# The product that turns the log-sums is laid out without the margin behind its rows

## The chip, the cores and the metric

The kernel runs on one core of one Trainium2 chip. The metric is the device time of one execution in microseconds; the other seven cores are idle. "PE" is the engine of the matrix products, "PEld" its weight loads, DVE, ACT and POOL the vector, scalar and general engines, SP the queue that issues transfers.

## The reference, cut to what matters

Two attention layers with separate inputs, side by side in the output. Each has 2048 positions, width 1024 and 32 heads of 32 columns; all numbers are float32.

```
def _B_ref(x, wqkv, wo):                       # "dense" here: a window of 256 keys
    q, k, v = ... (x @ wqkv) in 32 heads of 32
    scores = einsum("bhqd,bhkd->bhqk", q, k) * 32 ** -0.5
    mask = 0 <= query - key < 256
    p = softmax(where(mask, scores, -1e9))
    o = einsum("bhqk,bhkd->bhqd", p, v)
    return o @ wo

def _A_ref(x, wqkv, wo):                       # 8 keys per query, every second position
    ...
return concatenate([a, b], axis=-1)
```

Layer B is the one that the change concerns.

## The kernel before

The work is cut into eight units of 512 positions: units 0 to 3 are layer B (dense), units 4 to 7 layer A (window). A unit has eight groups of four heads; the 32 groups of the dense units are numbered 0 to 31 below (group = 8 x unit + number in the unit). All products of the projections are made of three products of rounded parts, high x high, high x low and low x high (`TERMS`), each 128 x 128 by 128 x 512 (or 256); they are the products named `g` in the profile and the bulk of PE's work.

A dense group goes twice over its scores, in products named `s` on a ring of four banks (`rs`):

- First pass (`first`, 16 products `s<-kst,qst`, queries on the partitions). DVE masks each product and takes its minimum after a change of sign (`nm`, line 1323), ACT exponentiates and sums (`sm`, line 1328). After the 16th, `log_sum` takes the logarithm on ACT (`ln`, line 1341), and DVE forms `nl` = `nm` - `ln` and splits it into a high and a low part (`hl`, lines 1346 to 1349).
- The product that turns the log-sums (`rows`): one product `s<-ident,hl` of `hl` with an identity. It brings the 128 x 32 numbers onto 32 partitions. Four DVE operations (line 1363, `spread`) write them, one for each head, as 32 more rows under the queries (`qst`, partitions 96 to 127). The matching rows of the keys hold ones, so that the second pass subtracts the log-sum in the product itself.
- Second pass (`second`, products `s<-qst,kst`, keys on the partitions). ACT exponentiates straight into `pbuf`, POOL or DVE mask it (`keep`, lines 1387 and 1390), and products named `o` multiply it with the values.

The order on every engine is written at build time by a planner. It keeps a model clock (`Clock`, `ck`) with a time at which each engine comes free, and has four lists: `aux` (the turning products alone), `ones` (first passes), `twos` (second passes and values) and `gemm` (the `g` products). At each step the item whose `ready()` is earliest goes to PE next, and `aux` wins a tie. Work for the other engines is put into their queues when the model clock reaches it; a `keep` goes to POOL or DVE, and a cast of weights to ACT or DVE, whichever the model has free first. On the chip each engine's instructions keep that order and wait for semaphores, so that the model's times decide nothing but the order. The item of `rows` is entered in `parts` with the condition that a bank of `rs` is free and that the model's end of `hl`, `e2`, has passed by a margin:

```
HL_LATE = 0.8
...
e2 = ck.use("dve", 0.52, e, port=True)
aux.append(Item(lambda: latest(rs.when(BANK_LATE), e2 + HL_LATE), lambda: rows(hl), 0.08))
```

The times of `spread`, and with them those of the second pass, are counted from the place where the turning product was laid.

Of the kernel before, what the change touches and what calls it, by code (L numbers as in the profile page):

```python
# [29 lines left out]
CHUNK, ASKED, LEFT, FETCHED = 256, 150, 290, 7.0  # L30
EXTRA, EACH = 246, 5.2
P_LATE = 1.5
HL_LATE = 0.8
VPARTS = ((0,4),(4,2),(6,2))
V_SLOTS = {0:0,5:1,7:2}
O_SLOTS = {2: (0, 1), 3: (2, 3), 4: (4, 5), 5: (6, 7)}
# [17 lines left out]
BANK_LATE = 0.0  # L54
# [189 lines left out]
def kernel(ctx, tc, xs, wqk, wv, wo, outs, units):  # L244
# [26 lines left out]
    def mm(out, left, right, **k):  # L271
        issued[0] += 4 if left.dtype == F32 else 2
        n = int(issued[0] + EXTRA - ASKED) // CHUNK
        if n > asked[0]:
            asked[:] = n, ck.now
        nc.tensor.matmul(out, left, right, **k)  # L276
# [195 lines left out]
    xt, xready, ot, rows, waiting = {}, {}, {}, {}, {}  # L472
# [24 lines left out]
    rg, rs, ro = Ring(psg, 7 - NS, "g"), Ring(pss, NS, "s"), Ring(pso, 1, "o")  # L497
# [7 lines left out]
    def latest(*ts):  # L505
        return None if any(t is None for t in ts) else max(ts)
# [788 lines left out]
    def attention(u, s):  # L1295
# [43 lines left out]
        def log_sum():  # L1339
            ln = small.tile([P, 16], F32, tag="ln", name="ln")  # L1340
            nc.scalar.activation(ln, h["sm"], AF.Ln)
            e = ck.use("act", 0.13, ck.now) - 0.03

            def parts():
                nl = small.tile([P, 16], F32, tag="nl", name="nl")
                nc.vector.tensor_tensor(nl, h["nm"], ln, op=ALU.subtract)
                hl = small.tile([P, 2, 16], F32R, tag="hl", name="hl")
                nc.vector.tensor_copy(hl[:, 0, :], nl)
                nc.vector.tensor_tensor(hl[:, 1, :], nl, hl[:, 0, :].bitcast(F32), op=ALU.subtract)
                e2 = ck.use("dve", 0.52, e, port=True)  # L1350
                aux.append(Item(lambda: latest(rs.when(BANK_LATE), e2 + HL_LATE), lambda: rows(hl), 0.08))

            ck.defer(e, parts)

        def rows(hl):
            ps, bank = rs.take()
            mm(ps[0:32, 0:P], hl.rearrange("p a b -> p (a b)"), cst["ident"], start=True, stop=True)

            def spread():

                h["rows"] = []
                for j in range(4):
                    nc.vector.tensor_tensor(q[96:P, j, :].rearrange("p (b s) -> p b s", s=P),  # L1363
                                            ps[0:32, None, 0:P].to_broadcast([32, 4, P]),
                                            cst["pick"][0:32, 4 * j:4 * j + 4, None].to_broadcast([32, 4, P]), op=ALU.mult)
                    e = ck.use("dve", 0.61, ck.now)
                    h["rows"].append(e + ROWS_LATE)
                rs.give(bank, e)

            return spread  # L1370
# [102 lines left out]
    aux, ones, twos, gemm = [], [], [], []  # L1473
# [121 lines left out]
```

## Time and profile before

| | us |
|---|---|
| median of 3 runs | 1811.09 (1808.05 to 1811.22) |
| the profiled execution | 1810.36 |
| its span, from the first to the last instruction | 1808.5 |
| PE busy | 1779.4 (98% of the span) |
| DVE, ACT, POOL busy | 1294.4, 935.2, 417.7 |
| granted clock of PE, mean | 0.998 |

A PE that is called busy may still be late: its products overlap, and their ends are modelled. What counts is when the next product starts. "Idle before" in a row is the time that an engine stood still ahead of the instructions of the group, with what ended it. Of the 1.9 us between span and time nothing is seen in the profile.

### The profile page before, as it was taken

The numbers are of one execution on the slowest core, as the hardware profiler recorded it, in microseconds if no ns is written. First come the engines' busy times: TensorE is split into PE (matmuls) and PEld (weight loads), VectorE is DVE, ScalarE is ACT, GpSimd is POOL, SyncE is SP. The second block draws the span as 40 slices with busy tenths as digits, with TensorE's granted clock in tenths as the row PEclk, the third lists the DMA queues.
The fourth block names the chain that finished last, engine by engine and source line by source line (L and its number), as shares of the span: only waits on it lengthen the run. The fifth ranks groups of instructions, "written<-read, shape, count | busy, mean of one in ns | idle before, by whom it ended". The sixth has DMA issues, their size and how long they took to land. (4 is left out here: it accounts for less than half of the span.)

```text
span 1808.5 us, 38436 instructions
## 1 busy us (share of the span) xinstructions
PE 1779.4 (98%) x14490; PEld 1439.0 (80%) x14490; DVE 1294.4 (72%) x2879; ACT 935.2 (52%) x2319; POOL 417.7 (23%) x967
## 2 busy tenths in 40 slices
PE   9999999999999999999999999999999999999999
PEld 7787778888777888777788788878887777887887
DVE  6777877768767668866678476665666768678866
ACT  5566466555666565655654543434443435356442
POOL 2323322232333233232324400110011101001220
PEclk9999999999999999999999999999999999999999
DMA  8455665645655556555556266666576568858984
GB/s 241 120 146 126 183 165 146 163 141 140 184 140 150 159 135 165 152 146 141 142 133 182 63 207 180 203 207 192 172 214 200 180 191 275 259 178 283 333 291 148
DMA packets 154649, 324.57 MB, mean 179 GB/s; under 512 B 18016, under 2 KB 58976, under 8 KB 154464
## 3 DMA queue, kind: packets, MB, share of 16 engines
q0 software_dynamic: 45792, 166.74, 30.5%
q1 hardware_dynamic: 97728, 134.40, 26.5%
q10 hardware_dynamic: 10944, 20.98, 3.1%
q8 instruction: 115, 1.88, 0.4%
q14 instruction: 70, 0.57, 0.1%
HBM read 201.33 MB, written 53.48 MB: 141 GB/s over the span
## 5 line engine op out<-in xcount | busy, mean ns | idle before, releaser
L276 PE MATMUL g<-x,w 128*128 128x512 f32 x3744 | 928.5, 395 | 5.1 <-ACT x L228 2.0
L276 PEld LDWEIGHTS g<-x,w 128*128 128x128 f32 x3744 | 692.0, 189 | 145.2 <-issue 5.6
L234 DVE TENSOR_TENSOR w<-raw,w 128x512 fp32r<-128x512 f32 x510 | 334.6, 697 | 51.7 <-ACT w L228 45.6
L276 PE MATMUL g<-w,x 128*128 128x256 f32 (+1 forms) x1872 | 332.8, 327 | 0.9 <-DVE w L234 0.7
L1323 DVE CUSTOM_DVE_ANT_0 s<-s,mask_d 128x384 f32<-128x384 f32 (+2 forms) x512 | 262.1, 553 | 98.1 <-PE s L276 96.8
L1328 ACT ACTIVATE s<-s,nm 128x384 f32<-128x384 f32 (+2 forms) x512 | 274.8, 538 | 101.4 <-DVE nm L1323 99.3
L276 PEld LDWEIGHTS g<-w,x 128*128 128x128 f32 x1872 | 276.7, 190 | 28.1 <-DVE w L234 2.2
L1387 POOL TENSOR_SCALAR_AFFINE_SELECT pbuf<-pbuf 128x128 f32<-128x128 f32 (+1 forms) x619 | 226.0, 393 | 300.9 <-ACT pbuf L1408 299.5
L1408 ACT ACTIVATE pbuf<-s 128x384 f32<-128x384 f32 (+2 forms) x480 | 202.7, 505 | 88.6 <-PE s L276 87.1
L276 PE MATMUL g<-r,w 128*128 128x512 f32 x768 | 190.8, 394 | 1.5 <-DVE r L1287 0.8
L276 PEld LDWEIGHTS g<-r,w 128*128 128x128 f32 x768 | 141.9, 188 | 30.9 <-DVE r L1287 1.8
L183 POOL DMA_DIRECT2D raw<-wqk x126 | 68.0, 540 | 417.2 <-DVE w L234 267.4
L276 PEld LDWEIGHTS s<-qst,kst 128*128 128x128 f32 x704 | 112.2, 189 | 43.6 <-ACT s L1328 17.7
L276 PE MATMUL s<-kst,qst 96*128 96x384 f32 (+2 forms) x512 | 142.9, 343 | 3.7 <-ACT s L1328 1.1
L231 DVE CAST w<-raw 128x1024 fp32r<-128x1024 f32 x176 | 122.1, 694 | 27.2 <-PE g L276 26.8
L276 PE MATMUL s<-qst,kst 128*128 128x256 f32 (+2 forms) x704 | 136.6, 302 | 4.6 <-ACT s L1328 3.5
L228 ACT CAST w<-raw 128x1024 fp32r<-128x1024 f32 (+1 forms) x80 | 82.7, 1038 | 75.8 <-PE g L276 29.0
L276 PEld LDWEIGHTS s<-kst,qst 96*128 96x128 f32 x512 | 92.9, 189 | 29.4 <-issue 6.1
L1328 ACT ACTIVATION_READ_ACCUMULATOR s<-s,nm 128x1 f32 x512 | 105.9, 207 | 0.0
L1190 ACT COPY wide<-band 32x512 f32<-32x512 f32 x128 | 79.0, 617 | 46.4 <-DVE band L1181 44.6
L276 PE MATMUL o<-pbuf,vbuf 128*32 128x384 f32 (+2 forms) x1408 | 91.1, 389 | 0.0
L1363 DVE TENSOR_TENSOR qst<-s,pick 32x512 fp32r<-32x512 f32 x128 | 79.3, 676 | 12.8 <-PE s L276 12.0
(90 smaller groups left out, 1327.7 us busy)
## 6 DMA issues: line engine op xcount, KB each, us to landing
raw<-wqk POOLq DMA_DIRECT2D x126, 512.0 KB, 4.6
raw<-wv POOLq DMA_DIRECT2D x60, 512.0 KB, 5.2
qst<-nat SPq DMA_DIRECT2D x96, 256.0 KB, 4.2
kst<-nat SPq DMA_DIRECT2D x96, 256.0 KB, 5.6
raw<-wo POOLq DMA_DIRECT2D x44, 512.0 KB, 4.9
raw<-xs POOLq DMA_DIRECT2D x28, 512.0 KB, 4.9
outs<-ost ACTq DMA_DIRECT2D x38, 256.0 KB, 2.8
kst<-halo SPq DMA_DIRECT2D x72, 128.0 KB, 4.5
```

The source lines that it names most:

```text
L183: (self.nc.scalar if early else self.nc.gpsimd).dma_start(raw if len(ap.shape) == 2 else raw.rearrange("p (a b) -> p a b", a=2), ap)
L228: nc.scalar.copy(t[:, 0, :], raw)
L231: nc.vector.tensor_copy(t[:, 0, :], raw)
L234: nc.vector.tensor_tensor(t[:, 1, c:c + 512], raw[:, c:c + 512], t[:, 0, c:c + 512].bitcast(F32), op=ALU.subtract)
L276: nc.tensor.matmul(out, left, right, **k)
L1190: nc.scalar.copy(diag[r:r + 32, :, :, c:c + 32], turned[r:r + 32, :, :, 1, :])
L1323: nc.vector.tensor_tensor_reduce(ps[:, :n], ps[:, :n], mask[:, cut:full], scale=-1.0, scalar=BIG, op0=ALU.add, op1=ALU.min, accum_out=nm)
L1328: nc.scalar.activation(ps[:, :n], ps[:, :n], AF.Exp, bias=nm, scale=-1.0, accum_out=sm)
L1363: nc.vector.tensor_tensor(q[96:P, j, :].rearrange("p (b s) -> p b s", s=P), ps[0:32, None, 0:P].to_broadcast([32, 4, P]), cst["pick"][0:32 ...
L1387: nc.gpsimd.affine_select(w, w, pattern=[[0, m], [step, n]], compare_op=ALU.is_ge, fill=0.0, base=base, channel_multiplier=chan)
L1408: nc.scalar.activation(w, ps[:, :pack * n].rearrange("p (j n) -> p j n", j=pack), AF.Exp)
```

## The change

The margin goes: the turning product may be laid down as soon as the model has `hl` ready.

```
-HL_LATE = 0.8
...
-                aux.append(Item(lambda: latest(rs.when(BANK_LATE), e2 + HL_LATE), lambda: rows(hl), 0.08))
+                aux.append(Item(lambda: latest(rs.when(BANK_LATE), e2), lambda: rows(hl), 0.08))
```

Line numbers from 33 on fall by one. No product is added or left out; the order shifts from the first turning product on. On PE the first 184 and the last 5,748 of 11,164 instructions of the order stand as before; on SP all do. On DVE there are 15 more instructions and on POOL 13 fewer, because a `keep` finds another engine free first: on 128 x 2 x 128 elements DVE makes 58 of them in place of 40 and POOL 166 in place of 184; on 128 x 128 DVE makes 72 in place of 77 and POOL 440 in place of 435. One cast of weights and one copy of values go from ACT to DVE.

PE at group 4, from the group's last product of the first pass (`kst_124,qst_122`, the third row of each piece) to the turning product; `kst_125,qst_123` are the scores of group 5. Before:

```order
L276 MATMUL s<-kst_124,qst_122 128x384
L276 MATMUL g<-x,w 128x512 x3
L276 MATMUL s<-kst_124,qst_122 128x384
L276 MATMUL g<-x,w 128x512 x15
L276 MATMUL s<-kst_125,qst_123 128x128 x2
L276 MATMUL g<-x,w 128x512 x3
L276 MATMUL s<-kst_125,qst_123 128x128 x2
L276 MATMUL g<-x,w 128x512 x9
L276 MATMUL s<-kst_125,qst_123 128x256 x3
L276 MATMUL g<-x,w 128x512 x3
L276 MATMUL s<-ident,hl 32x128
```

Now:

```order
L275 MATMUL s<-kst_124,qst_122 128x384
L275 MATMUL g<-x,w 128x512 x3
L275 MATMUL s<-kst_124,qst_122 128x384
L275 MATMUL g<-x,w 128x512 x9
L275 MATMUL s<-kst_125,qst_123 128x128 x4
L275 MATMUL g<-x,w 128x512 x9
L275 MATMUL s<-kst_125,qst_123 128x256
L275 MATMUL s<-ident,hl 32x128
L275 MATMUL g<-x,w 128x512 x3
```

Between the last score of group 4 and its turning product stood 30 `g` products and seven small scores; now there are 18 and five.

PE at group 9 (`kst_125,qst_123`), and what follows the turning product. Before:

```order
L276 MATMUL s<-kst_125,qst_123 128x384 x2
L276 MATMUL g<-r,w 128x512 x27
L276 MATMUL s<-kst_124,qst_122 128x384 x4
L276 MATMUL g<-r,w 128x512 x6
L276 MATMUL s<-ident,hl 32x128
L276 MATMUL g<-r,w 128x512 x3
```

Now:

```order
L275 MATMUL o<-pbuf,vbuf_126 32x128 x4
L275 MATMUL s<-kst_125,qst_123 128x384
L275 MATMUL g<-r,w 128x512 x18
L275 MATMUL s<-ident,hl 32x128
L275 MATMUL g<-r,w 128x512 x9
```

Here 33 `g` products and four scores of the next group are cut to 18 `g` products.

PE at group 22 (`kst_124,qst_122`), where it goes the other way. Before:

```order
L276 MATMUL s<-kst_124,qst_122 128x384
L276 MATMUL g<-x,w 128x512 x6
L276 MATMUL s<-kst_124,qst_122 128x384
L276 MATMUL g<-x,w 128x512 x6
L276 MATMUL s<-ident,hl 32x128
```

Now:

```order
L275 MATMUL o<-pbuf,vbuf_127 32x128 x4
L275 MATMUL s<-kst_124,qst_122 128x384
L275 MATMUL g<-x,w 128x512 x12
L275 MATMUL s<-ident,hl 32x128
```

Six `g` products have become twelve: the schedule around it has shifted by more than the margin. Over all 32 groups the turning product stands nearer to its group's last score in 18, farther in 10 and at the same distance in 4.

## The prediction

> **What bounds the kernel now.** I read the page first, then the kernel in stretches, then the waits of PE in the dense part, then the turning product itself.
>
> ```profile
> PE 1779.4 (98%) x14490; PEld 1439.0 (80%) x14490; DVE 1294.4 (72%) x2879; ACT 935.2 (52%) x2319; POOL 417.7 (23%) x967
> ```
>
> PE has something running for 1779.4 of 1808.5 us, and the change gives it the same products in another order. So the time can change only by as much as PE's standing still changes. The order on PE is as before from the last 5,748 instructions back, and those are the window units and the end. What moves lies between the first scores and the last dense group. Those stretches, with the columns PE, PEld, DVE, ACT, POOL (busy us and instructions), granted clock, share of the DMA engines and GB/s:
>
> ```profile
> 32.00:290.00 258.00, 252.39 (x1465) 200.75 (x1464) 197.94 (x549) 149.65 (x464) 77.36 (x190) 1.00 0.57 152
> 290.00:540.00 250.00, 248.18 (x1542) 200.99 (x1541) 188.61 (x481) 146.22 (x418) 70.91 (x175) 1.00 0.56 157
> 540.00:790.00 250.00, 246.85 (x1516) 199.88 (x1515) 184.48 (x463) 143.51 (x411) 77.66 (x192) 1.00 0.56 150
> 790.00:1035.00 245.00, 242.94 (x1501) 196.93 (x1500) 169.25 (x423) 141.50 (x400) 84.32 (x209) 1.00 0.49 135
> ```
>
> Over these 1003 us PE is busy for 252.39 + 248.18 + 246.85 + 242.94 = 990.4 us. It is idle for 12.6 us by this count, so no removal of a wait can bring much over 12 us, while a new wait in PE's in-order queue costs its whole length. DVE is the next engine, at 740.3 of 1003 us. Who makes PE and its weight loads wait in this part (total us, times, longest):
>
> ```profile
> PE s L276 <- ACT s L1328: 4.6, 7, 1.1
> PE s L276 <- DVE hl L1349: 3.7, 3, 1.5
> PE s L276 <- DVE qst L1363: 1.3, 3, 0.5
> PEld s L276 <- ACT s L1328: 22.3, 44, 1.6
> PEld s L276 <- ACT ln L1341: 4.9, 3, 1.9
> PEld s L276 <- ACT pbuf L1408: 1.4, 5, 0.5
> ```
>
> With the margin in place, the turning product is already the second largest waiter of PE: 3 of 32 wait for `hl`, 3.7 us in all. Group 5 is the clearest. In the timeline (start, length, engine and line) its three last scores begin at 174.81:
>
> ```profile
> 174.81 1.20 PE L276 MATMUL s<-kst,qst 96*128 96x384 f32 x3
> 176.83 0.96 PE L276 MATMUL g<-x,w 128*128 128x512 f32 x3
> 178.26 0.22 ACT L1341 ACTIVATE ln<-sm 128x16 f32<-128x16 f32 x1
> 178.93 0.17 DVE L1349 TENSOR_TENSOR hl<-nl,hl 128x16 fp32r<-128x16 f32 x1
> 179.21 0.11 PEld L276 LDWEIGHTS s<-ident,hl 128*32 128x32 f32 x1 [1.86 <-ACT ln L1341]
> 179.25 0.22 PE L276 MATMUL s<-ident,hl 128*32 128x128 f32 x1 [1.46 <-DVE hl L1349]
> 179.30 1.65 PE L276 MATMUL g<-w,x 128*128 128x256 f32 x12
> 179.51 2.48 DVE L1363 TENSOR_TENSOR qst<-s,pick 32x512 fp32r<-32x512 f32 x4 [0.41 <-PE s L276]
> ```
>
> PE ran out at 177.79, `hl` ended at 179.10, and its weight load began 0.11 us later. The twelve `g` products, which need nothing of it, stood behind it for the 1.46 us, and their weight loads too.
>
> **The change part by part.** The step of a `g` product comes from a row at group 9, between two kinds of scores:
>
> ```profile
> 296.03 6.32 PE L276 MATMUL g<-r,w 128*128 128x512 f32 x27
> 302.19 0.86 PE L276 MATMUL s<-kst,qst 96*128 96x384 f32 x4
> ```
>
> (302.19 - 296.03) / 27 = 0.228 us; a score of 384 columns takes (302.89 - 302.19) / 4 = 0.175 by the next row's start, below.
>
> *The turning product comes earlier.* I call the time from the end of `hl` to the weight load of its product the slack. The ends are the first of the 32 and the last; between them groups 4 and 9:
>
> ```profile
> 49.77 0.18 DVE L1349 TENSOR_TENSOR hl<-nl,hl 128x16 fp32r<-128x16 f32 x1
> 51.79 0.11 PEld L276 LDWEIGHTS s<-ident,hl 128*32 128x32 f32 x1
> 160.98 0.18 DVE L1349 TENSOR_TENSOR hl<-nl,hl 128x16 fp32r<-128x16 f32 x1
> 162.15 0.11 PEld L276 LDWEIGHTS s<-ident,hl 128*32 128x32 f32 x1
> 301.52 0.17 DVE L1349 TENSOR_TENSOR hl<-nl,hl 128x16 fp32r<-128x16 f32 x1
> 302.89 1.54 PE L276 MATMUL g<-r,w 128*128 128x512 f32 x6
> 304.04 0.11 PEld L276 LDWEIGHTS s<-ident,hl 128*32 128x32 f32 x1
> 1016.70 0.18 DVE L1349 TENSOR_TENSOR hl<-nl,hl 128x16 fp32r<-128x16 f32 x1
> 1016.93 0.11 PEld L276 LDWEIGHTS s<-ident,hl 128*32 128x32 f32 x1
> ```
>
> The slacks are 1.84, 0.99, 2.35 and 0.05 us. Over all 32 they run from 0.05 to 3.43 us, with 1.3 in the middle: three stand at the 0.11 to 0.12 us of a waiting one (groups 5, 6 and 22), three between 0.7 and 0.81, seven between 0.97 and 1.04, the others above. Two ways to carry them over:
>
> - If each product came just 0.8 us earlier against its `hl`, the three waiting ones would wait 0.8 us more each, group 31 some 0.87 us (0.12 + 0.8 - 0.05), and the three below 0.81 about 0.2, 0.2 and 0.1 us: 3 x 0.8 + 0.87 + 0.5 = 3.8 us more.
> - By the distances in the new order, with each `hl` as late after its last score as now, the shift of a group is the change of its distance. Group 4 loses 12 `g` products and two scores of 128 x 256, 12 x 0.228 + 2 x 0.12 = 3.0 us (0.12 is 256/384 of the 0.175), and waits 3.0 - 0.99 + 0.12 = 2.1 us. Group 9 loses 15 `g` and four scores, 15 x 0.228 + 4 x 0.175 = 4.1 us, and waits 1.9 us. Group 6 (3 `g` fewer) waits 0.7 us longer; groups 14 (six fewer), 17 and 25 wait 0.7, 0.4 and 0.4 us. Group 5 keeps its distance and its wait; group 22 gets six `g` more and stops waiting, a gain of about 1.3 us. Sum: 2.1 + 1.9 + 0.7 + 0.7 + 0.4 + 0.4 - 1.3 = 4.9 us more.
>
> For group 9 the second way is an upper bound, since DVE's and ACT's queues in front of its `ln` move as well. I take 4.2 us, between the two. The ends are -3.7 us, all of today's wait gone, and +12 us, a wait like the longest here (1.5 us) in eight groups more. What is queued behind such a wait is every later product of PE. Who waits for it is `spread` on DVE, and behind `spread` the casts that feed the next `g` products; 2.48 us of `spread` stand there in either order.
>
> *The second pass starts earlier.* The rows under the queries are written earlier by about as much as the product moved, and the second scores after them. PE has `g` products to fill with until then, so nothing is won on PE directly; I take 0. What could be won is in the 4.6 + 1.3 us that scores wait on PE for a bank or for `qst`; what could be lost is the same kind again. The ends are -5 and +5 us.
>
> *Bursts on the ring.* I counted, in both orders, the products of the ring that take a bank less than 0.8 us of PE work after the second-pass score that last held it: 9 before, 14 now. Their cost is in the row of the waits for `pbuf`, 1.4 us in all. 1.4 x 14 / 9 - 1.4 = 0.8 us more. Its ends are 0 and 3 us.
>
> *Masks and casts change engine.* Their rows, with shapes, count, busy us and mean ns:
>
> ```profile
> L1387 POOL TENSOR_SCALAR_AFFINE_SELECT pbuf<-pbuf 128x128 f32<-128x128 f32 x435 | 139.5, 351 | 150.1 <-ACT pbuf L1408 150.0
> L1387 POOL TENSOR_SCALAR_AFFINE_SELECT pbuf<-pbuf 128x256 f32<-128x256 f32 x184 | 87.6, 491 | 150.8 <-ACT pbuf L1408 149.6
> L1390 DVE TENSOR_TENSOR pbuf<-pbuf,keep_d 128x128 f32<-128x128 f32 x43 | 13.3, 308 | 15.6 <-ACT pbuf L1408 15.4 <-POOL pbuf L1387 0.2
> L1390 DVE TENSOR_TENSOR pbuf<-pbuf,keep_d 128x256 f32<-128x256 f32 x20 | 8.6, 443 | 20.5 <-ACT pbuf L1408 20.4
> L231 DVE CAST w<-raw 128x1024 fp32r<-128x1024 f32 x176 | 122.1, 694 | 27.2 <-PE g L276 26.8
> ```
>
> DVE gets 18 x 0.443 - 5 x 0.308 + 2 x 0.694 = 7.8 us more (the copy taken at the cast's price), POOL 18 x 0.491 - 5 x 0.351 = 7.1 us less. DVE is free for 263 of the 1003 us, so it fits; if it had no cover it would cost at most the 7.8 us. I take 0.
>
> The sum, on the profiled execution's own 1810.36 us: 4.2 + 0.8 = 5.0 us, 1815.4 us. That execution is 0.7 us below the median of 1811.09 and is taken as it is.
>
> The clock shows 1.00 in all four stretches, with waits of up to 1.5 us in them, so I put nothing on it. The Trainium skill ("TensorE: Matmul & The Clock Gate", Part 1) has a rule that speaks against the change: after an idle window of about 3.4 us the clock falls to half. Our waits stay under that length, and whether it holds no run here shows; it is the last rival.
>
> **The rivals.**
>
> - *The queues move along (no change).* `hl` is made by DVE and ACT in an order that the same planner lays, and 14 of the 32 products come no nearer at all. By distances the 32 together come nearer by only 7 us. If today's 3.7 us stay 3.7 us, the time is 1810.4 us. Against it: the 3 products that wait do so although the margin is there.
> - *Faster.* The second pass comes off the ring sooner, first and second scores lie less on top of each other, and the waits for ACT shrink. The weight loads of scores wait 22.3 us for ACT, the largest item. If the 5.9 us of PE go and `hl` gains nothing: 1810.4 - 5.9 = 1804.5 us. For it: at group 9 the next group's four first scores no longer stand ahead of the turning product. Against it: PE is busy while it waits for most of the 22.3 us. It decides if the turning product costs no more than now.
> - *Much slower.* A late turning product holds `spread`, `spread` holds DVE's queue, and the next casts come late for the `g` products. It decides when about eight products wait as long as the longest here: 8 x 1.5 = 12 us, 1822.4 us. Against it: PE waits for casts hardly at all in the dense part now.
> - *The clock falls.* Two waits of 3.4 us, each 1.9 us longer than the longest now, and after each a stretch at half speed: the ten filler products of 512 columns with which the program begins (row below) take 4.6 / 10 = 0.46 us each in place of 0.228, so that a stretch of 3.4 us at that speed loses 1.7. 2 x (1.9 + 1.7) = 7.2 us on top of the forecast, 1822.6 us.
>
> ```profile
> L276 PE MATMUL s<-qst 128*128 128x512 f32 x10 | 4.6, 645 | 1.5 <-DVE qst L1512 1.5
> ```
>
> **How the numbers follow.** A measurement of this kernel can tell about 0.2%, 3.6 us, from no change: faster is below 1807.5, slower above 1814.7 us. The forecast has 0.54; its 1815.4 lies just above the bound, and with its terms' ends it runs from 1811 to 1821, so that 0.10 of the 0.54 is "same". No change has 0.12 (0.10 "same", 0.02 slower). Faster has 0.22, of which 0.02 is "same". Much slower has 0.10 and the clock 0.02. So slower is 0.44 + 0.02 + 0.12 = 0.58, same 0.10 + 0.10 + 0.02 = 0.22, faster 0.20. The range goes from 1805.5, which keeps about half of the faster cases, to 1822.0, which leaves out most of the last two; the forecast alone is 1811 to 1821.
>
> **What would show it.** In the profile after: the waits of PE for `hl` should rise from 3.7 to about 8 us, in 6 to 8 products, groups 4, 5 and 6 among them and 22 not; the waits for `pbuf` to about 2 us; DVE's busy time by about 8 us; the stretches after the dense part should be as long as now. The forecast is wrong if the dense part ends earlier than now, if `hl` still costs under 4 us, or if the time went into another row of PE's waits than these.

## The result and the profile after

| | before | after |
|---|---|---|
| median of 18 runs, us | 1810.78 (1805.82 to 1814.47) | 1806.04 (1802.74 to 1809.90) |
| the profiled execution, us | 1810.36 | 1805.95 |
| its span, us | 1808.5 | 1804.2 |

The ratio is 0.9976, with a 95% interval of 0.9968 to 0.9983: faster by 0.24%, or 4.7 us, where 5.0 us more were forecast. In the kernel after, every line stands one lower than in the one before (line 275 is 276 of before, 1348 is 1349).

The page of the kernel after:

```profile
PE 1777.3 (99%) x14490; PEld 1439.5 (80%) x14490; DVE 1300.4 (72%) x2894; ACT 934.8 (52%) x2317; POOL 412.0 (23%) x954
```

The same 14,490 products; DVE is 6.0 us busier, POOL 5.7 us less busy. The same four stretches of after, columns as before:

```profile
32.00:290.00 258.00, 252.95 (x1465) 201.57 (x1464) 198.76 (x555) 151.61 (x469) 74.81 (x183) 1.00 0.54 150
290.00:540.00 250.00, 248.83 (x1544) 201.40 (x1544) 186.60 (x472) 146.08 (x417) 77.43 (x192) 1.00 0.56 156
540.00:790.00 250.00, 248.81 (x1534) 202.59 (x1533) 190.05 (x478) 146.82 (x421) 77.93 (x192) 1.00 0.55 154
790.00:1035.00 245.00, 243.49 (x1517) 196.67 (x1516) 173.14 (x431) 137.49 (x390) 77.55 (x194) 1.00 0.49 135
```

PE is busier in each stretch, and in the third it starts 18 products more in the same 250 us. The granted clock in these stretches is 1.00 as before. The boundaries of the dense part, first score and last dense `o`, are these in the timeline of before:

```profile
32.77 0.56 PE L276 MATMUL s<-kst,qst 96*128 96x128 f32 x4
...
1036.52 1.50 PE L276 MATMUL o<-pbuf,vbuf 128*32 128x384 f32 x24
```

and in that of after:

```profile
31.45 0.56 PE L275 MATMUL s<-kst,qst 96*128 96x128 f32 x4
...
1028.59 1.87 PE L275 MATMUL o<-pbuf,vbuf 128*32 128x384 f32 x24
```

From the first score to the start of the last of those `o` it is 1005.0 us before and 998.7 after, 6.3 us less. The start ahead of it is 1.4 us shorter and the rest behind it 3.2 us longer (770.8 and 774.0 us). Both have the same order in the two kernels, and over the twelve experiments below they vary between 30.2 and 33.1 and between 770.1 and 775.7 us. Run 11, whose order on PE is that of before, has 1004.9 us between. So the 6.3 us are what the change moves; the other two are the spread of single executions. The longer rest shows in one place of after: a `g` product there waits 1.94 us for its weights, where the same product waited 0.19 us before, and 3.41 us at half the clock follow (last section). Below, "dense part" is this length. Waits of PE and of its weight loads there, after:

```profile
PE s L275 <- ACT s L1327: 3.6, 5, 1.1
PE s L275 <- DVE hl L1348: 3.1, 4, 2.0
...
PEld s L275 <- ACT s L1327: 19.9, 41, 1.6
PEld s L275 <- ACT ln L1340: 4.7, 4, 2.4
PEld s L275 <- ACT pbuf L1407: 2.6, 10, 0.5
```

Rows of before that had smaller numbers than those shown with the prediction, and that are gone after:

```profile
PE s L276 <- DMA halo<-nat: 0.7, 1, 0.7
PE s L276 <- DMA kst<-nat: 0.6, 1, 0.6
```

PE's waits in scores fell by 4.6 - 3.6 = 1.0 us for ACT, 1.3 for `qst`, 0.7 + 0.6 for transfers, and by 3.7 - 3.1 = 0.6 for `hl`: 4.2 us. Those in `g` products rose by 0.9 us. A second count does not rest on modelled ends. For each product I took the distance to the next product's start less what that step usually is (the 40th percentile for its tile and shape in before), and added it up by the tile that starts late:

| late in the dense part, us | before | after |
|---|---|---|
| first scores | 12.1 | 8.5 |
| second scores | 22.3 | 19.0 |
| turning products | 4.3 | 3.7 |
| all products | 124.8 | 118.5 |

The last row must fall by the 6.3 us of the dense part, since the products are the same; how it divides is what the count tells. The scores fall by 6.9 us (3.6 + 3.3), the turning products by 0.6, and the others rise by 1.2. (The levels hang on which step is taken as usual; the differences hardly do.) By units 0.9 of the 6.9 us lie in units 0 and 1, 6.0 in units 2 and 3. The turning product, on which the forecast rested, hardly counts.

What such a wait looks like is seen at group 17. PE and DVE, before (the turning product is at 560.84):

```profile
557.89 0.86 PE L276 MATMUL s<-kst,qst 96*128 96x384 f32 x4
559.74 0.69 DVE L231 CAST w<-raw 128x1024 fp32r<-128x1024 f32 x1
560.46 1.29 DVE L234 TENSOR_TENSOR w<-raw,w 128x512 fp32r<-128x512 f32 x2
560.84 0.22 PE L276 MATMUL s<-ident,hl 128*32 128x128 f32 x1
563.35 2.48 DVE L1363 TENSOR_TENSOR qst<-s,pick 32x512 fp32r<-32x512 f32 x4
565.97 0.41 PE L276 MATMUL s<-kst,qst 96*128 96x384 f32 x1 [0.54 <-DVE qst L1363]
```

Scores of the next group stand ahead of the turning product. `spread`, which empties its bank, has a split and those scores' masks before it in DVE's queue and starts 2.3 us after the product. The score at 565.97 takes that bank in its turn on the ring and waits for the end of `spread` (563.35 + 2.48 = 565.83). After:

```profile
557.40 0.22 PE L275 MATMUL s<-ident,hl 128*32 128x128 f32 x1
557.46 0.73 PE L275 MATMUL s<-kst,qst 96*128 96x384 f32 x3
557.66 2.48 DVE L1362 TENSOR_TENSOR qst<-s,pick 32x512 fp32r<-32x512 f32 x4 [0.86 <-PE s L275]
...
565.88 0.52 PE L275 MATMUL s<-kst,qst 96*128 96x384 f32 x2
```

The turning product goes first, `spread` starts at once, and no score waits for it. The same pair stands at group 25.

### The profile page after: what moved, and what is told of

It is laid out like the page before. It is cut to its first block, busy times and chain, and to the rows that moved or that the text cites. A ratio compares the mean times of both kernels' runs of the same rounds, so it can differ in the third digit from the quotient of the medians.

```text
span 1804.2 us, 38469 instructions
## 1 busy us (share of the span) xinstructions
PE 1777.3 (99%) x14490; PEld 1439.5 (80%) x14490; DVE 1300.4 (72%) x2894; ACT 934.8 (52%) x2317; POOL 412.0 (23%) x954
## 5 line engine op out<-in xcount | busy, mean ns | idle before, releaser
L1386 POOL TENSOR_SCALAR_AFFINE_SELECT pbuf<-pbuf 128x128 f32<-128x128 f32 (+1 forms) x606 | 220.7, 392 | 324.0 <-ACT pbuf L1407 322.6
L1150 DVE TENSOR_TENSOR band<-s,near 128x160 f32<-128x160 f32 x128 | 32.4, 316 | 79.6 <-PE s L275 79.5
```

The source lines that it names most:

```text
L1150: nc.vector.tensor_tensor(p64()[:, j, :, 24:], banks[j][0][:, :160].rearrange("p (b c) -> p b c", b=4), m, op=ALU.add)
L1386: nc.gpsimd.affine_select(w, w, pattern=[[0, m], [step, n]], compare_op=ALU.is_ge, fill=0.0, base=base, channel_multiplier=chan)
```

## The experiments

Three theories. *Place*: the gain comes because the turning product and `spread` stand earlier. *Order*: it comes from where the other products, the scores, have come to stand, and the earlier turning product by itself costs. *Masks*: it comes from the masks that went to DVE. All ratios are against the kernel before on the same chip in five rounds; before was at 1809.24, 1809.46 and 1810.67 us in the three sets (1 to 4, 5 to 8, 9 to 12).

**1. Before, with the turning product alone moved earlier**, by one item of `g` (three products) in 22 groups (by the trace in 23, in one of them by two items).

```
+ hold[0] = name == "g" and pos["a"] < 32     # a g item's products are kept back
  after = it.run()
+ if name == "a" or ...: let_go()             # the turning product goes out ahead of them
```

> The kernel before, order of every engine kept, but the turning product stands one item of g products (three, about 0.69 us) earlier in 22 of the 32 groups. Theory 'place' (the gain of the change comes from the turning product and the spread behind it standing earlier): about two thirds of the gain, 1807.5 us, ratio 0.998 to the kernel before, and the waits of scores on PE fall as in the changed kernel. Theory 'order' (the gain comes from where the other products came to stand; the turning product itself only costs when it is earlier): no gain, 1811 to 1814 us, ratio 1.000 to 1.002, waits of PE for hl up from 3.7 us to 5 or more, the waits of scores for qst, halo and kst still there.

1812.09 us, 1.0019 (1.0008 to 1.0029). Waits of PE in its dense part:

```profile
PE s L286 <- ACT s L1338: 5.7, 11, 1.1
PE s L286 <- DVE hl L1359: 3.7, 3, 1.9
```

The late starts of turning products rise from 4.3 to 6.8 us, and the waits for ACT from 4.6 to 5.7. The row for `hl` stays at 3.7, where 5 or more was expected: the wait of group 22 rises from 1.17 to 1.89 us, but that of group 6 (1.05) is missing. It is missing in runs 9 and 10 too, whose order there is that of before, so that such a row of one execution is good to about 1 us only. *Place* falls: earlier by itself brings nothing, and by the median it costs 2.8 us. Where these lie the profile doesn't show: the dense part is 1006.5 us, 1.5 more than before, and holds 3.41 us at half the clock.

**2. After, with the turning product alone moved later**, behind the next item in all 32 groups.

```
+ hold[0] = name == "a"
  after = it.run()
+ hold[0] = False
+ if name != "a": let_go()
```

> The changed kernel, order of every engine kept, but the turning product stands behind the next item in all 32 groups (three g products in most, a score in 11). Theory 'place': most of the gain is given back, 1808 to 1810 us, ratio 0.999. Theory 'order': the gain stays or grows by what is left of the waits for hl (3.1 us): 1803 to 1806 us, ratio 0.996 to 0.998.

1804.62 us, 0.9978 (0.9966 to 0.9991). The waits for `hl` fall to:

```profile
PE s L275 <- DVE hl L1358: 1.3, 1, 1.3
```

The gain stays, and does not grow, with the turning product back behind other work. Both runs say *order*.

**3 and 4. Margins of 0.4 and 1.2 in place of 0.8 and 0.**

```
-HL_LATE = 0.8
+HL_LATE = 0.4      # 3;  4: 1.2
```

> The margin at 0.4 us, the planner lays the rest anew. Theory 'place': half way, 1808.4 us, ratio 0.9988. Theory 'order': another draw of the order, anywhere from 1804 to 1815 us, with no place between the two kernels due to it.

> The margin at 1.2 us. Theory 'place': as much slower than the kernel before as 0.4 us of margin are worth, 1813 us, ratio 1.0012. Theory 'order': anywhere from 1804 to 1815 us; waits for hl close to nothing in both theories.

1815.92 us, 1.0039 (1.0026 to 1.0053), and 1815.94 us, 1.0033 (1.0020 to 1.0046). Half the margin is slower than either end, and so is more of it. Both lie just above the 1815 us that *order* had allowed. Their waits, at 0.4:

```profile
PE s L276 <- ACT s L1328: 5.0, 8, 1.2
PE s L276 <- DVE hl L1349: 3.3, 2, 2.1
PE s L276 <- DMA kst<-nat: 1.9, 1, 1.9
```

and at 1.2:

```profile
PE s L276 <- ACT s L1328: 4.5, 8, 1.0
PE s L276 <- DMA kst<-nat: 2.6, 2, 1.8
PE s L276 <- DVE qst L1363: 2.6, 6, 0.9
```

At 1.2 `hl` still costs 1.8 us, where close to nothing was expected. But `hl` cost 3.7 us before and is not what makes the two slower; more waits for transfers at both, and for `qst` at 1.2, are in these rows. The number itself has no direction: it re-lays the schedule, and each schedule has its own waits. At 0.4 the dense part is 1009.0 us, 4.0 more than before, with 3.41 us at half the clock in it (up to 1.7 us of the 4.0), and the median granted clock of its runs is 0.996 against 0.998 of before. At 1.2 the dense part is 1006.3, so that most of that loss does not lie there in the one execution profiled, and is left open.

**5 and 6. The margin gone in units 2 and 3 alone, or in units 0 and 1 alone.**

```
- latest(rs.when(BANK_LATE), e2 + HL_LATE)
+ latest(rs.when(BANK_LATE), e2 + (0.0 if u > 1 else HL_LATE))      # 5;  6: u < 2
```

> The margin is dropped for the groups of units 2 and 3 alone (16 to 31). PE's order is then that of the kernel before up to group 15 and that of the changed kernel from group 20 on. The waits of scores on PE fell in the changed kernel by 0.9 us in units 0 and 1 and by 6.0 us in units 2 and 3. Theory 'order' (the gain lies in where the scores stand, and so is where those waits fell): most of the gain, 1806 to 1807.5 us, ratio 0.9975 to 0.9985. Theory 'place', which e1 speaks against already: half the gain, 1808.4 us, ratio 0.9988.

> The margin is dropped for the groups of units 0 and 1 alone (0 to 15). PE's order is that of the changed kernel up to group 15 and that of the kernel before from group 24 on, with groups 16 to 23 as neither has them. Theory 'order': little of the gain, 1809 to 1812 us, ratio 0.999 to 1.001. Theory 'place': half the gain, ratio 0.9988.

1805.36 us, 0.9974 (0.9964 to 0.9983), and 1810.31 us, 1.000 (0.999 to 1.001). The whole gain is in units 2 and 3, where the late starts of scores had shrunk.

**7. After, with each mask on the engine that it had before** (133 of 736 masks differ); the planner still counts its own choice, so that PE, ACT and SP keep the order of after.

```
+ on_pool = ck.ends("pool", dur_p, r) <= ck.ends("dve", dur_d, r, port=True) + MASK_BIAS
- if ck.ends("pool", dur_p, r) <= ck.ends("dve", dur_d, r, port=True) + MASK_BIAS:
+ if key not in DVE_KEEPS:          # the list of before
```

> The changed kernel with the order of PE, ACT and SP kept, but each mask on the engine that makes it in the kernel before (133 of 736 change between DVE and POOL; DVE has 13 instructions fewer than in the changed kernel). Theory 'order': the gain stays, 1805 to 1807 us, ratio 0.997 to 0.9985. Theory 'masks' (the gain comes from masks that DVE ends sooner than POOL, 0.443 against 0.491 us on the wide ones): it goes, 1809 to 1811 us, ratio 0.9995 to 1.0005.

1809.25 us, 1.000 (0.9989 to 1.0012). *Order* was wrong here: the gain is lost. Its waits show a part of what took it:

```profile
PE s L277 <- DMA halo<-nat: 1.8, 1, 1.8
PE s L277 <- DMA r<-wv: 0.8, 1, 0.8
PE s L277 <- DMA kst<-nat: 0.5, 1, 0.5
```

These 3.1 us are not in after's rows, and the dense part is 1004.1 us, 5.4 more than after's. The largest wait is at 728 us, for keys and their halo that SP had asked for over 10 us earlier:

```profile
714.19 2.88 SPq L593 DMA_DIRECT2D kst<-nat  x3
717.12 0.84 SPq L583 DMA_DIRECT2D halo<-nat  x1
728.36 0.66 PE L277 MATMUL s<-kst,qst 96*128 96x384 f32 x1 [1.77 <-DMA halo<-nat]
```

The same place in after, whose schedule is 0.9 us ahead there (its turning product of group 22 starts at 718.94, here at 719.84):

```profile
713.22 2.69 SPq L591 DMA_DIRECT2D kst<-nat  x3
725.27 0.34 PE L275 MATMUL s<-kst,qst 96*128 96x384 f32 x1
```

From issue to landing the three transfers of keys took 10.5 to 11.8 us here and 8.4 to 8.7 in after; over all 14 profiles the same three took 5.3 to 11.8. Behind the wait come 3.41 us at half the clock (last section). POOL, whose queue the masks changed, asked for a piece of weights at 710.92 us, in after at 708.35, which against the schedule is some 1.7 us later. That this is what held the keys up is not shown.

**8. Before, with another constant of the planner changed:** the bias between POOL and DVE for masks, the margin kept.

```
-MASK_BIAS = 0.2
+MASK_BIAS = 0.3
```

> The margin as before, but a constant that has nothing to do with the turning product is moved a little: the model's bias for masks on POOL from 0.2 to 0.3 us, which sends the order another way. Theory 'order': a shift of several us to either side, as large as that of the change, 1804 to 1816 us. If the time stayed within 1 us of the kernel before, a new order alone would not explain the gain.

1805.86 us, 0.9976 (0.9967 to 0.9985). A constant that has nothing to do with the turning product gives the same gain.

**9 and 10. The margin gone in single groups:** 17 and 25, or 20 and 28.

```
+ (0.0 if u > 1 and s == 1 else HL_LATE)      # 9;  10: s == 4
```

> The kernel before with the margin dropped for groups 17 and 25 alone. On PE the turning product then stands ahead of one score of the next group and three g products; on DVE the spread stands ahead of that score's masking; little else moves, and nothing outside these two places. Theory 'order', in its narrow form: the bank of the turning product comes free sooner, and the two waits of a first-pass score for qst (0.70 us each at 566 and 825 us) are gone: 1.4 us, ratio 0.9992, the rest of PE's waits as before. If those waits stay or others of the same size take their place, the narrow form is wrong.

> The kernel before with the margin dropped for groups 20 and 28 alone, whose turning product then stands ahead of the next group's scores; the order of groups 20 to 22 and from 28 on changes with it, groups 0 to 19 and 24 to 27 stay. Theory 'order': the waits that lie there (1.07 us twice for ACT, 1.34 us for hl at 724, 0.36, 0.47 and 0.46 us) shrink or go, 2 to 4 us, ratio 0.998 to 0.999; the two of 0.70 us at groups 17 and 25 stay.

Groups 17 and 25: 1809.44 us, 0.9995 (0.9986 to 1.0004), which can't be told from nothing. The wait for `spread`'s bank is gone, but the second scores, which need `spread` as well, now come so early that they wait themselves, at 564 and at 823 us. By their late starts the two waits are halved (0.70 to 0.35 us each) and not gone, as the narrow form had it. At 564 us:

```profile
563.27 0.84 PE L276 MATMUL g<-x,w 128*128 128x512 f32 x3
564.31 0.41 PE L276 MATMUL s<-qst,kst 128*128 128x128 f32 x2 [0.20 <-DVE qst L1363]
```

Groups 20 and 28: 1807.21 us, 0.9984 (0.9975 to 0.9993). There a second score waits for ACT at 713 us. Before:

```profile
713.60 1.38 PE L276 MATMUL s<-qst,kst 128*128 128x256 f32 x6 [0.90 <-ACT s L1328]
```

and in this run:

```profile
713.31 0.82 PE L276 MATMUL s<-qst,kst 128*128 128x128 f32 x4 [0.61 <-ACT s L1328]
```

That wait shrinks, and so does its twin in unit 3; three later ones in unit 3 (758, 1005 and 1020 us, 0.36 to 0.47 us by their late starts) are gone. So is the largest of those expected to shrink, the 1.17 us that group 22's turning product waited for `hl` at 724 us. The waits for `qst` at groups 17 and 25 stay. These two groups bring 3.5 us by the medians, of the 4.1 (1809.46 - 1805.36) that units 2 and 3 bring in run 5; by the ratios it is 0.16% of 0.26%.

**11. Before, with each mask on the engine of after:** the edit of run 7 the other way round.

> The kernel before with the order of PE, ACT and SP kept, but each mask on the engine that makes it in the changed kernel (the reverse of e7). Theory 'masks': the gain of the change, 1805 to 1807 us, ratio 0.9975. Theory 'order', with e7's loss put down to masks that no longer fit the order that was planned for them: no gain, ratio 1.000 to 1.002.

1810.90 us, 1.0007 (0.9996 to 1.0017). *Masks* falls: on the order of before they bring nothing. With run 7: the order of after needs its own masks, and they are worth nothing without it.

**12. Both constants,** margin 0 and bias 0.3.

> Both constants: no margin, and the bias for masks at 0.3 us. If the two gains of 4 to 5 us were causes of their own they would add, 1801 us, ratio 0.995. Theory 'order': another draw, 1803 to 1812 us, with no reason to add.

1806.41 us, 0.9977 (0.9969 to 0.9986). The two gains do not add. None of the twelve is measurably faster than after; the lowest ratio, 0.9974 in run 5, has an interval that covers 0.9976.

## Why the prediction was wrong

- **What bounds the kernel** was right: the products stayed the same, the time moved only by PE's late starts, and all of what the change did lies in the dense part.
- **"The turning product comes earlier"** was mis-sized: +4.2 us forecast, and `hl` costs 0.6 us less, not more. The products did come nearer to their `hl`: the slack in the middle went from 1.29 to 0.57 us. But four wait in place of three, and not for longer in sum. The sign holds only when nothing else moves: in run 1 turning products start 2.5 us later in all, and the time rises by 2.8 us. In the change itself, the step "with each `hl` as late after its last score as now" failed. At group 9 the forecast was a wait of up to 1.9 us. Before, ACT's queue had a copy of finished outputs between the group's exponentials, which itself waited for its `g` products:

```profile
297.87 0.55 ACT L1328 ACTIVATE s<-s,nm 128x384 f32<-128x384 f32 x1
...
299.67 0.59 ACT L659 COPY ost<-g 128x512 f32<-128x512 f32 x1 [1.14 <-PE g L276]
300.15 0.56 ACT L1328 ACTIVATE s<-s,nm 128x384 f32<-128x384 f32 x1
...
300.86 0.21 ACT L1341 ACTIVATE ln<-sm 128x16 f32<-128x16 f32 x1
```

  In after the exponentials follow one another, and the logarithm comes right behind them (the timeline of all engines):

```profile
294.20 4.28 PE L275 MATMUL g<-r,w 128*128 128x512 f32 x18
295.74 0.55 ACT L1327 ACTIVATE s<-s,nm 128x384 f32<-128x384 f32 x1
296.44 0.22 ACT L1340 ACTIVATE ln<-sm 128x16 f32<-128x16 f32 x1
297.10 0.18 DVE L1348 TENSOR_TENSOR hl<-nl,hl 128x16 fp32r<-128x16 f32 x1
298.31 0.22 PE L275 MATMUL s<-ident,hl 128*32 128x128 f32 x1
```

  From the first product behind the last score to the end of `hl` it was 301.69 - 296.03 = 5.7 us, and is 297.28 - 294.20 = 3.1. The product came 4.1 us of work earlier and still did not wait; nor did group 4. The waiting groups are 5, 6, 14 and 22. So 5, 6 and 14 were named rightly, but not their sizes: 5, which was to keep its wait, went from 1.46 to 1.99 us, and 6, which was to wait longer, from 1.05 to 0.50. And 22, which was to stop, still waits 0.5 us by its late start.
- **"The second pass starts earlier", taken at 0,** is the step that failed most: late starts of scores fell by 6.9 us, past its lower end of -5. I had treated the rest of the order as neutral, where 34.4 us of late scores (12.1 + 22.3) stood that a new order can redeal.
- **"Bursts on the ring"** was right as to its row: `pbuf` waits of weight loads went from 1.4 to 2.6 us, 2.2 forecast. PE's own waits for `pbuf` stayed at 0.3 us, so that no cost on PE shows.
- **"Masks and casts change engine"**: DVE +6.0 and POOL -5.7 us (7.8 and 7.1 forecast), at no cost of their own. But that they could be counted apart from the order was wrong (run 7).
- **Rivals.** *Faster* came: 1804.5 us forecast, 1806.04 measured. Its place was right, its list only in part: waits for `qst` went (1.3 us), those for ACT fell by 1.0 of 4.6, and 1.3 us came from transfers it didn't name. *The clock falls* did not come in after's dense part, where all four stretches stand at 1.00 and the longest wait for `hl` is 2.0 us. But its condition of 3.4 us was wrong: in six of the twelve experiments' profiles the clock falls to half in the dense part, behind 1.2 to 2.0 us of standing still (last section). The Trainium skill ("TensorE: Matmul & The Clock Gate", Part 1) puts the fall to half behind an idle window of about 3.4 us. The traces agree with it on the half, and differ on how much idle time it takes; the measurement decides.
- **Open.** Which single score wait is worth how much (run 9 is below what five rounds can tell); why the masks of before bring late transfers in the order of after; most of the loss at a margin of 1.2.

## What to carry to other kernels

Where a planner lays the order of every engine, a constant in it is not priced by the instruction that it names: compare the two whole orders and price the work that got displaced, starting with the engine that bounds. Price the engines that make the operand in the new order too, since the operand's lateness is not a constant. When another constant gives the same gain, and a value in between gives a loss, it is a lucky schedule that was found and not a mechanism; search such constants by timing them, and expect the best value to change with the next edit.

## What was not expected of the hardware

With the same products on PE, order alone and the choice of engine for masks moved the time between 0.9974 and 1.0039 of before, 0.65% or some 12 us from end to end. Parts whose order is the same in all kernels differ from execution to execution by almost as much as the change brings: the start by 2.9 us and the rest behind the dense part by 5.6 us. A single profile's span would therefore not have settled the sign.

Much of that spread goes with the granted clock. Of the 26 executions of before beside runs 1 to 4, the three with a mean of 1.000 took 1805.5 to 1805.8 us, and the six with 0.996 took 1811.1 to 1814.4. In the traces the clock is full or half, and half lasts 3.41 us or twice that. The start takes 30.2 us without such a piece, 31.4 to 32.2 with one of 3.41 us and 32.6 to 33.1 with 6.83 us. Behind the start the 14 profiles have 18 such pieces, six of them in the dense part (runs 1, 3, 6, 7, 9 and 10). In the 3.41 us ahead of each, PE had stood still for 1.2 to 2.0 us in all. The piece in the rest of after, with the stretch ahead of it, and the one of run 7 (columns as before, clock third from the end):

```profile
1341.50:1344.90 3.40, 1.46 (x7) 0.66 (x6) 3.33 (x6) 3.05 (x7) 0.00 (x0) 1.00 0.44 158
1345.00:1348.30 3.30, 3.30 (x27) 2.17 (x29) 1.40 (x4) 2.77 (x5) 0.70 (x1) 0.50 0.45 107
728.30:731.50 3.20, 3.14 (x8) 2.78 (x9) 3.01 (x9) 0.80 (x3) 1.29 (x2) 0.50 0.53 194
```

In such a piece a `g` product of 512 columns takes 0.427 us in place of 0.228, so that one piece costs up to 1.7 us, by this estimate from its length. A wait of over one us on PE can thus cost up to 1.7 us more than its own length, but it does so only in some executions: group 5 waits 1.99 us for `hl` in after and in runs 6 and 7, in the same order, and the clock falls behind it in run 6 alone. The gain itself is not the clock's: the median granted clock is 0.997 in after's runs and 0.997 to 0.998 in the three sets of before.
